# A new instruction order for a spectral filter plus gated feed-forward kernel, with the identity loaded first and a longer warm-up

## The chip, the cores and the metric

The kernel runs on one core of one Trainium2 chip. The metric is the device time of one execution in microseconds, and lower is better. Six executions of the kernel before took 203.97, 203.63, 202.84, 203.64, 203.67 and 202.80 us, so the median is 203.64 us.

## The reference

The input x has 2048 rows of 640 numbers. It is normalised by row, and the normalised matrix goes through two branches that are added to x:

```python
def _A_ref(x, w_r, w_i):
    X = rfft2(x.astype(float32), axes=(-2, -1))     # 2048 x 321 complex
    X = X * (w_r + 1j * w_i)
    return irfft2(X, s=(S, D), axes=(-2, -1)).astype(bfloat16)

def _B_ref(x, w_gate, w_up, w_down):                # F = 1536
    g = einsum("bsd,df->bsf", x, w_gate)
    u = einsum("bsd,df->bsf", x, w_up)
    return einsum("bsf,fd->bsd", g * u, w_down)

xn = _layernorm(A_x)
return A_x + _A_ref(xn, A_w_r, A_w_i) + _B_ref(xn, B_w_gate, B_w_up, B_w_down)
```

## The kernel before

**Steps.** The rows are cut into 16 blocks of 128. The kernel creates 1021 named steps, each a few instructions of one engine, and the names return in the prediction:

- `ld_x`, `ld_gw`, `ld_sm0`, `ld_w`, `ld_wd`, `ld_xr`, `st_out` are loads and stores (line 679 issues all of them). `ld_sm0` is a 128x128 identity matrix, `ld_gw0_1` the first part of the up weights and `ld_gw0_0` that of the gate weights, `ld_w` the filter weights, `ld_wd` the down weights.
- `warm` (L720) and `fill` (L709) on TensorE multiply zeros; nothing reads their results.
- Normalisation: `bn`, `ag` on VectorE for blocks 0 to 5, `sm`, `sq` (L738, L747) on ScalarE for blocks 6 to 15; `sd` takes the square root on ScalarE (L774/775), `rs` the reciprocal on VectorE (L782), `sub` and `mul` apply it.
- `T0` (L818) transposes blocks 0 to 3 on TensorE with the identity, `eT0` copies the result out; the other blocks are transposed by DMA (L806).
- Feed-forward: `GU` multiplies by gate and up weights (L968 for narrow pieces, L948 for pieces of 512 rows), `eG` copies the result from PSUM, `H` multiplies gate and up on VectorE (L984/985), `ACC` multiplies by the down weights (L1206).
- Spectral branch: `S1` to `S5` on VectorE are additions of the forward transform; `R` (L908), `D` (L1026), `C` (L1049) are its products on TensorE, with evictions `eR` and `eD`; `WM` multiplies by the filter on VectorE (three instructions, L1064 and L1067); `NG` and `NS` (L1076/1077, L1084 to 1086) lay out negated copies; `IA` (L1100/1101) and `I` (L1129) are products of the inverse, with evictions `eIA` and `eI`; `V1` to `V5` are its additions on VectorE; `IV` (L1218) adds the last product into the PSUM bank of an `ACC`. `FINA` and `FIN` (L1245, L1227) bring the bank out and add x.

All copies out of PSUM go through one helper, so ScalarE's have line 685 and VectorE's line 686.

**Dependencies that matter.** `D` needs every `eR`, each `R` of a group needs `S5` of that group, `I` needs every `eIA`. A TensorE step that takes one of the eight PSUM banks waits until the step that read the bank's former content is done.

**What sets the order.** The order of the program is not that of the Python loops. `_PLAN` is a fixed list of triples (step number, engine, PSUM bank), made outside of this file. `replay` goes through the list, gives each step to the engine named and each TensorE step its bank; `compute_waits` then derives the semaphore waits. The durations passed to each step only enter the replay's own estimate of times, which decides how waits are merged; they are not instructions. Each engine runs its own list strictly in order, so a step whose input is late holds up everything behind it on that engine. SyncE issues nearly all DMAs in one such list; ScalarE's list begins with two DMAs.

Of the kernel before, what the change touches and what calls it, by code (L numbers as in the profile page):

```python
# [399 lines left out]
def _d_act(n):  # L400
# [4 lines left out]
    (14, 4, -1), (178, 1, -1), (8, 2, -1), (21, 2, -1), (20, 2, -1), (22, 2, -1), (15, 4, -1), (9, 3, -1), (0, 1, -1),  # L405
    (23, 1, -1), (25, 2, -1), (24, 2, -1), (26, 2, -1), (177, 4, -1), (13, 0, 0), (31, 2, -1), (30, 2, -1), (179, 4, -1),
    (180, 4, -1), (16, 4, -1), (27, 0, 2), (11, 0, 4), (32, 2, -1), (28, 1, -1), (12, 0, 5), (33, 1, -1), (17, 4, -1),
    (29, 2, -1), (189, 0, 6), (35, 2, -1), (34, 2, -1), (10, 0, 7), (36, 2, -1), (37, 0, 0), (39, 2, -1), (181, 4, -1),
    (187, 0, 7), (190, 1, -1), (188, 1, -1), (194, 0, 4), (182, 4, -1), (38, 2, -1), (40, 2, -1), (192, 0, 5), (41, 2, -1),
    (199, 0, 2), (183, 4, -1), (191, 2, -1), (42, 2, -1), (197, 0, 3), (195, 1, -1), (202, 0, 4), (43, 1, -1), (50, 2, -1),  # L410
    (45, 2, -1), (184, 4, -1), (44, 2, -1), (46, 2, -1), (193, 1, -1), (49, 2, -1), (198, 1, -1), (204, 0, 5), (47, 0, 3),
    (196, 2, -1), (51, 2, -1), (209, 0, 6), (52, 1, -1), (200, 1, -1), (203, 1, -1), (48, 1, -1), (54, 2, -1), (53, 2, -1),
    (55, 2, -1), (18, 4, -1), (56, 0, 7), (205, 1, -1), (201, 2, -1), (207, 0, 0), (57, 1, -1), (214, 0, 1), (120, 2, -1),
    (206, 2, -1), (212, 0, 7), (121, 2, -1), (217, 0, 2), (185, 4, -1), (210, 1, -1), (208, 1, -1), (70, 1, -1), (211, 2, -1),
    (122, 2, -1), (215, 1, -1), (62, 2, -1), (219, 0, 3), (58, 2, -1), (61, 2, -1), (213, 1, -1), (59, 2, -1), (63, 2, -1),
    (60, 2, -1), (123, 2, -1), (186, 4, -1), (216, 2, -1), (71, 1, -1), (72, 1, -1), (64, 1, -1), (224, 0, 4), (1, 4, -1),
    (19, 4, -1), (222, 0, 5), (220, 1, -1), (218, 1, -1), (2, 4, -1), (65, 2, -1), (124, 2, -1), (229, 0, 6), (73, 1, -1),
    (127, 0, 0), (125, 0, 2), (66, 2, -1), (221, 2, -1), (129, 2, -1), (227, 0, 7), (225, 1, -1), (223, 1, -1), (68, 2, -1),
    (130, 2, -1), (230, 1, -1), (74, 1, -1), (128, 1, -1), (80, 1, -1), (228, 1, -1), (234, 0, 4), (81, 1, -1), (226, 2, -1),
    (82, 1, -1), (232, 0, 5), (83, 1, -1), (131, 2, -1), (231, 2, -1), (237, 0, 6), (233, 1, -1), (75, 2, -1), (3, 4, -1),  # L420
    (84, 1, -1), (235, 1, -1), (132, 2, -1), (239, 0, 7), (76, 2, -1), (78, 2, -1), (4, 4, -1), (238, 1, -1), (240, 1, -1),
    (85, 2, -1), (5, 4, -1), (126, 1, -1), (6, 4, -1), (7, 4, -1), (90, 1, -1), (242, 0, 0), (244, 0, 1), (243, 1, -1),
    (133, 2, -1), (67, 4, -1), (245, 1, -1), (91, 1, -1), (134, 0, 4), (136, 0, 6), (236, 2, -1), (247, 0, 2), (249, 0, 3),
    (69, 4, -1), (77, 4, -1), (92, 1, -1), (250, 1, -1), (248, 1, -1), (86, 2, -1), (241, 2, -1), (93, 1, -1), (94, 1, -1),
    (254, 0, 0), (252, 0, 1), (138, 2, -1), (79, 4, -1), (100, 1, -1), (246, 2, -1), (139, 2, -1), (253, 1, -1), (101, 1, -1),
    (255, 1, -1), (259, 0, 3), (251, 2, -1), (257, 0, 2), (140, 2, -1), (256, 2, -1), (88, 2, -1), (264, 0, 1), (258, 1, -1),
    (95, 2, -1), (87, 4, -1), (262, 0, 0), (102, 1, -1), (260, 1, -1), (269, 0, 2), (103, 1, -1), (135, 1, -1), (104, 1, -1),
    (141, 2, -1), (261, 2, -1), (96, 2, -1), (263, 1, -1), (142, 2, -1), (265, 1, -1), (267, 0, 3), (272, 0, 4), (274, 0, 5),
    (268, 1, -1), (270, 1, -1), (98, 2, -1), (105, 2, -1), (273, 1, -1), (266, 2, -1), (89, 4, -1), (106, 2, -1), (275, 1, -1),
    (97, 4, -1), (149, 0, 0), (108, 2, -1), (277, 0, 3), (137, 1, -1), (271, 2, -1), (143, 0, 4), (110, 1, -1), (150, 1, -1),  # L430
    (99, 4, -1), (147, 0, 6), (278, 1, -1), (282, 0, 2), (144, 1, -1), (151, 2, -1), (283, 1, -1), (279, 0, 0), (280, 1, -1),
    (276, 2, -1), (145, 0, 4), (287, 0, 1), (284, 0, 0), (152, 2, -1), (111, 1, -1), (289, 0, 3), (281, 2, -1), (285, 1, -1),
    (153, 2, -1), (112, 1, -1), (286, 2, -1), (290, 1, -1), (288, 1, -1), (113, 1, -1), (154, 2, -1), (114, 1, -1), (292, 0, 2),
    (291, 2, -1), (294, 0, 3), (115, 2, -1), (155, 2, -1), (299, 0, 0), (293, 1, -1), (146, 1, -1), (297, 0, 1), (295, 1, -1),
    (148, 1, -1), (298, 1, -1), (118, 2, -1), (300, 1, -1), (156, 0, 4), (304, 0, 2), (302, 0, 3), (116, 2, -1), (296, 2, -1),
    (157, 1, -1), (164, 2, -1), (301, 2, -1), (307, 0, 6), (309, 0, 7), (160, 0, 0), (162, 0, 4), (303, 1, -1), (308, 1, -1),
    (107, 4, -1), (165, 2, -1), (305, 1, -1), (109, 4, -1), (158, 0, 2), (306, 2, -1), (117, 4, -1), (310, 1, -1), (314, 0, 6),
    (166, 2, -1), (119, 4, -1), (437, 4, -1), (161, 1, -1), (312, 0, 7), (319, 0, 0), (438, 4, -1), (311, 2, -1), (313, 1, -1),
    (163, 1, -1), (167, 2, -1), (439, 4, -1), (168, 2, -1), (315, 1, -1), (320, 1, -1), (159, 1, -1), (440, 4, -1), (441, 4, -1),
    (317, 0, 1), (316, 2, -1), (442, 4, -1), (318, 1, -1), (322, 0, 7), (324, 0, 6), (443, 4, -1), (175, 0, 4), (173, 0, 2),  # L440
    (174, 2, -1), (323, 1, -1), (327, 0, 7), (444, 4, -1), (169, 0, 0), (171, 0, 2), (176, 1, -1), (321, 2, -1), (325, 1, -1),
    (328, 1, -1), (329, 0, 4), (170, 2, -1), (445, 4, -1), (172, 1, -1), (446, 4, -1), (326, 2, -1), (449, 0, 5), (447, 0, 6),
    (330, 1, -1), (465, 0, 7), (450, 2, -1), (479, 4, -1), (463, 0, 0), (485, 0, 1), (466, 2, -1), (448, 1, -1), (487, 0, 2),
    (332, 0, 3), (451, 0, 4), (457, 0, 5), (334, 0, 6), (452, 2, -1), (464, 1, -1), (453, 3, -1), (467, 0, 7), (480, 4, -1),
    (486, 1, -1), (481, 4, -1), (473, 0, 4), (482, 4, -1), (501, 0, 0), (488, 1, -1), (339, 0, 1), (503, 0, 2), (454, 3, -1),
    (458, 2, -1), (335, 1, -1), (459, 1, -1), (337, 0, 5), (474, 2, -1), (333, 1, -1), (331, 2, -1), (468, 2, -1), (525, 0, 4),
    (475, 3, -1), (483, 4, -1), (460, 3, -1), (455, 0, 3), (484, 4, -1), (495, 0, 6), (745, 4, -1), (502, 1, -1), (469, 3, -1),
    (470, 3, -1), (504, 1, -1), (338, 2, -1), (517, 4, -1), (489, 0, 7), (456, 1, -1), (476, 3, -1), (342, 0, 0), (539, 0, 5),
    (461, 0, 2), (340, 1, -1), (496, 2, -1), (497, 3, -1), (523, 0, 3), (498, 3, -1), (336, 2, -1), (518, 4, -1), (343, 1, -1),
    (505, 0, 6), (344, 0, 1), (519, 4, -1), (462, 1, -1), (490, 2, -1), (520, 4, -1), (521, 4, -1), (511, 0, 0), (524, 2, -1),  # L450
    (522, 4, -1), (471, 0, 7), (477, 0, 2), (349, 0, 3), (526, 1, -1), (540, 1, -1), (541, 0, 4), (555, 4, -1), (491, 1, -1),
    (341, 2, -1), (472, 1, -1), (527, 0, 5), (492, 3, -1), (512, 2, -1), (533, 0, 0), (478, 1, -1), (514, 3, -1), (561, 0, 7),
    (506, 2, -1), (508, 3, -1), (507, 3, -1), (499, 0, 2), (345, 1, -1), (347, 0, 6), (528, 2, -1), (530, 3, -1), (556, 4, -1),
    (542, 1, -1), (557, 4, -1), (558, 4, -1), (559, 4, -1), (563, 0, 1), (579, 0, 5), (534, 2, -1), (493, 0, 4), (549, 0, 0),
    (348, 2, -1), (560, 4, -1), (500, 1, -1), (513, 3, -1), (352, 0, 2), (562, 1, -1), (494, 1, -1), (550, 2, -1), (509, 0, 4),
    (346, 2, -1), (593, 4, -1), (543, 0, 0), (577, 0, 7), (580, 2, -1), (544, 2, -1), (354, 0, 6), (529, 3, -1), (594, 4, -1),
    (515, 0, 5), (350, 1, -1), (535, 2, -1), (536, 3, -1), (601, 0, 3), (595, 4, -1), (564, 1, -1), (353, 1, -1), (571, 0, 2),
    (565, 0, 1), (551, 2, -1), (546, 3, -1), (578, 1, -1), (617, 0, 7), (355, 1, -1), (572, 2, -1), (596, 4, -1), (357, 0, 0),
# [69 lines left out]
def _build(nc, A_x, A_w_r, A_w_i, B_w_gate, B_w_up, B_w_down, out, opts=None):  # L528
    opts = opts or {}
    tabs = _build_tables()  # L530
    es = contextlib.ExitStack()
    with es:
# [171 lines left out]
        for fi in range(opts.get("nfill", 3)):  # L704
            def em_fill(c):
                bk = bank_of(c.t)
                ins = None
                for i in range(4):
                    ins = c.e.matmul(ps[:, bk, 64 * i:64 * i + 64], v_dum[:, 0:128], v_dum[:, 128:192], start=True,  # L709
                                     stop=True)  # L710
# [619 lines left out]
```

## Time and profile before

| | |
|---|---|
| median of 6 executions | 203.64 us |
| profiled execution, its own time | 202.85 us |
| its span, first to last instruction | 200.9 us |
| TensorE busy | 194.6 us (97%) |
| VectorE busy | 172.8 us (86%) |
| ScalarE busy | 128.4 us (64%) |
| GpSimd busy | 37.1 us (18%) |
| first x block landed | 3.5 us |
| first transpose on TensorE | 5.73 us |
| last matmul started | 198.4 us |

The busy times of the engines overlap, so they don't add up to the span. "PE" in the profile is TensorE's matmuls and "PEld" its weight loads, "DVE" is VectorE, "ACT" ScalarE, "POOL" GpSimd, "SPq" SyncE's DMA issues. Times of single instructions count from the start of the span.

### The profile page before, as it was taken

The numbers are of one execution on the slowest core, as the hardware profiler recorded it, in microseconds if no ns is written. First come the engines' busy times: TensorE is split into PE (matmuls) and PEld (weight loads), VectorE is DVE, ScalarE is ACT, GpSimd is POOL, SyncE is SP. The second block draws the span as 40 slices with busy tenths as digits, with TensorE's granted clock in tenths as the row PEclk, the third lists the DMA queues.
The fourth block names the chain that finished last, engine by engine and source line by source line (L and its number), as shares of the span: only waits on it lengthen the run. The fifth ranks groups of instructions, "written<-read, shape, count | busy, mean of one in ns | idle before, by whom it ended". The sixth has DMA issues, their size and how long they took to land.

```text
span 200.9 us, 4556 instructions
## 1 busy us (share of the span) xinstructions
PE 194.6 (97%) x1727; PEld 126.9 (63%) x1749; DVE 172.8 (86%) x396; ACT 128.4 (64%) x284; POOL 37.1 (18%) x116
## 2 busy tenths in 40 slices
PE   7799999999999999999999999999999999999995
PEld 7698644345445465666665566675677766777774
DVE  3899999999999889999969788799699998495813
ACT  3377999999776889999897955652436133312240
POOL 0000000000000009979836736000000000000000
DMA  6999984064028976454663000600024104241322
GB/s 175 303 328 378 382 122 83 0 68 98 0 53 252 193 234 128 109 134 123 154 161 80 17 5 0 206 26 0 6 74 149 38 0 131 65 134 46 121 98 65
DMA packets 29381, 23.81 MB, mean 119 GB/s; under 512 B 10288, under 2 KB 27312, under 8 KB 29232
## 3 DMA queue, kind: packets, MB, share of 16 engines
q1 hardware_dynamic: 28560, 23.16, 43.2%
q10 hardware_dynamic: 800, 0.36, 0.6%
q8 instruction: 14, 0.23, 0.5%
q14 instruction: 7, 0.06, 0.1%
HBM read 18.92 MB, written 2.62 MB: 107 GB/s over the span
## 4 chain that ended last, share of the span: by engine, by line
PE 63%; DVE 15%; ACT 8%; issue 5%; SPq 4%; DMA 4%
PE ps L1206 26%; PE ps L948 23%; ACT arena L685 5%; SPq L679 4%; DMA arena<-in_A_x_dram 4%; DVE arena L984 3%; PE ps L1100 2%; PE ps L1026 2%; PE ps L1101 2%; PE ps L1129 2%; PE ps L1218 2%; PE ps L1049 2%; DVE arena L861 2%; ACT arena L747 2%; ACT arena L738 2%
## 5 line engine op out<-in xcount | busy, mean ns | idle before, releaser
L685 ACT ACTIVATE arena<-ps 128x512 bf16<-128x512 f32 (+7 forms) x225 | 108.7, 528 | 58.0 <-PE ps L1218 30.1
L948 PE MATMUL ps<-arena 128*128 128x512 bf16 x398 | 94.7, 379 | 1.5 <-ACT arena L685 0.3
L948 PEld LDWEIGHTS ps<-arena 128*128 128x128 bf16 x420 | 39.4, 98 | 40.8 <-ACT arena L685 1.9
L1206 PE MATMUL ps<-arena 128*128 128x320 bf16 (+2 forms) x396 | 58.1, 295 | 0.0
L1206 PEld LDWEIGHTS ps<-arena 128*128 128x128 bf16 x396 | 37.7, 98 | 14.5
L1077 POOL TENSOR_SCALAR arena<-arena 128x256 bf16<-128x256 bf16 x15 | 12.9, 860 | 74.9 <-DVE arena L1067 74.9
L1064 DVE TENSOR_TENSOR arena<-ps,arena 128x256 bf16<-128x256 f32 x64 | 24.0, 417 | 2.2 <-PE ps L1049 2.0
L984 DVE TENSOR_TENSOR arena<-arena 128x512 bf16<-128x512 bf16 x42 | 17.9, 426 | 1.9 <-ACT arena L685 1.6
L686 DVE CAST arena<-ps 64x321 bf16<-64x321 f32 (+3 forms) x31 | 17.2, 555 | 2.6 <-PE ps L1101 0.9
L1245 DVE TENSOR_TENSOR arena<-arena 128x640 bf16<-128x640 bf16 x15 | 7.3, 490 | 10.8 <-ACT arena L685 10.8
L968 PE MATMUL ps<-arena 128*128 128x128 bf16 (+1 forms) x160 | 14.0, 246 | 0.6 <-ACT arena L775 0.6
L1100 PE MATMUL ps<-arena 128*128 128x64 bf16 x160 | 13.5, 196 | 0.1
L1101 PE MATMUL ps<-arena 128*128 128x64 bf16 x160 | 13.4, 197 | 0.0
L968 PEld LDWEIGHTS ps<-arena 128*128 128x128 bf16 x160 | 12.3, 98 | 1.7 <-DMA arena<-in_B_w_gate_dram 0.7
L1100 PEld LDWEIGHTS ps<-arena 128*128 128x128 bf16 x160 | 12.0, 114 | 1.7 <-DVE arena L686 0.3
L1086 POOL TENSOR_SCALAR arena<-arena 128x65 bf16<-128x65 bf16 x32 | 12.5, 390 | 0.0
L1101 PEld LDWEIGHTS ps<-arena 128*128 128x128 bf16 x160 | 11.3, 114 | 0.9
L1084 POOL COPY arena<-arena 128x63 bf16<-128x63 bf16 x32 | 8.4, 262 | 11.4 <-DVE arena L1067 11.3
L1026 PEld LDWEIGHTS ps<-arena 128*128 128x128 bf16 x160 | 7.4, 98 | 3.7 <-ACT arena L685 0.4
L1067 DVE TENSOR_TENSOR arena<-ps,arena 128x130 bf16<-128x130 f32 x32 | 9.3, 292 | 0.0
L1218 PE MATMUL ps<-arena 128*128 128x320 bf16 (+2 forms) x33 | 8.6, 295 | 0.0
L1026 PE MATMUL ps<-arena 128*128 128x64 bf16 (+1 forms) x160 | 8.5, 193 | 0.0
(63 smaller groups left out, 205.4 us busy)
## 6 DMA issues: line engine op xcount, KB each, us to landing
arena<-in_A_x_dram SPq DMA_DIRECT2D x20, 160.0 KB, 2.8
out_dram<-arena SPq DMA_DIRECT2D x15, 160.0 KB, 1.8
arena<-in_A_w_r_dram SPq DMA_DIRECT2D x8, 160.5 KB, 3.3
arena<-in_A_w_i_dram SPq DMA_DIRECT2D x8, 160.5 KB, 3.1
arena<-in_B_w_gate_dram SPq DMA_DIRECT2D x4, 320.0 KB, 5.4
arena<-in_A_x_dram SPq DMA_DIRECT2D x1, 1280.0 KB, 9.9
arena<-in_A_w_r_dram SPq DMA_DIRECT2D x14, 80.2 KB, 3.1
arena<-in_A_w_i_dram SPq DMA_DIRECT2D x14, 80.2 KB, 2.8
```

Of the source, the lines that this page charges most:

```text
L685: return c.e.activation(dst, src, _ACTF.Copy)
L686: return c.e.tensor_copy(dst, src)
L948: ins = c.e.matmul(ps[:, bk, :], v_gw[:, w, j, ft, :], v_xt[:, j, rows], start=(j == 0), stop=(j == 4))
L968: ins = c.e.matmul(ps[:, bk, w * n:(w + 1) * n], v_gw[:, w, j, ft, :], v_xt[:, j, rows], start=(j == 0), stop=(j == 4))
L984: return c.e.tensor_tensor(v_ht[:, ft0, rows], v_gbf[:, rr, 0, :], v_gbf[:, rr, 1, :], _OP.mult)
L1026: ins = c.e.matmul(ps[:, bk, k * 64:k * 64 + n], v_uq[:, k, t, :], v_fd[:, k * 128 + w * n: k * 128 + w * n + n], start=True, stop=True)
L1064: c.e.tensor_tensor(dst, xh.unsqueeze(1).to_broadcast([128, 2, 32, 4]), wv, _OP.mult)
L1077: return c.e.tensor_scalar(yg[:, 322:578], yg[:, 834:1090], -1.0, None, _OP.mult)
L1100: c.e.matmul(dst, l1, v_ti[:, q, 0, :], start=True, stop=False)
L1101: ins = c.e.matmul(dst, l2, v_ti[:, q, 1, :], start=False, stop=True)
L1206: ins = c.e.matmul(ps[:, bk, 0:sl3.stop - sl3.start], v_ht[:, ft, a * 128:(a + 1) * 128], v_wd[:, ft, sl3], start=(ft == _FT_ORDER[0]), st ...
L1218: return c.e.matmul(ps[:, bank_of(own), 0:sl3.stop - sl3.start], v_sm[:, 2, :], v_v[:, a, sl3], start=False, stop=True)
```

## The change

Outside of the plan the change is small. There are 40 warm-up matmuls instead of 36. Three filler steps of four small matmuls become one filler step of ten, and every narrow `GU` now depends on it. Four durations of the replay are corrected (`sd` 95 to 187 ns, `mul` 298 to 358 for blocks from 4 on, `NG` on GpSimd 1150 to 820, `warm` 4000 to 4280).

```diff
-        for fi in range(opts.get("nfill", 3)):
-            def em_fill(c):
-                bk = bank_of(c.t)
-                ins = None
-                for i in range(4):
-                    ins = c.e.matmul(ps[:, bk, 64 * i:64 * i + 64], v_dum[:, 0:128], v_dum[:, 128:192], start=True,
-                                     stop=True)
-                return ins
...
-        nwarm = opts.get("nwarm", 9)
+        nfill = opts.get("nfill", 10)
+
+        def em_fill(c):
+            bk = bank_of(c.t)
+            ins = None
+            for i in range(nfill):
+                ins = c.e.matmul(ps[:, bk, 64 * (i % 4):64 * (i % 4) + 64], v_dum[:, 0:128], v_dum[:, 128:192], start=True,
+                                 stop=True)
+            return ins
...
+        nwarm = opts.get("nwarm", 10)
...
-                gu = T("GU_%d_%d" % (ft, b0), "pe", 10.15 * _d_mm(n), em_gu,
+                gu = T("GU_%d_%d" % (ft, b0), "pe", 10.15 * _d_mm(n), em_gu, after=fills,
```

The plan is replaced as a whole; its first lines show the swap on ScalarE's list, where step 0 is `ld_sm0` and step 178 (176 after, since two fillers are gone) is `ld_gw0_1`. The other steps are the same, in another order. By the names of the steps, in the order in which the engines run them:

```
ScalarE before: ld_gw0_1 ld_sm0 sd_0 eT0_0 sd_1 eG_0_1 eG_0_0 eG_1_1 sd_2 ... eG_4_1 eG_4_0 sm6 eG_5_1 eG_5_0 sq6 sm7 sd_4 ...
ScalarE after:  ld_sm0 ld_gw0_1 sd_0 eT0_0 sd_1 eG_0_0 eG_0_1 eG_1_0 sd_2 ... eG_4_0 eG_4_1 eG_5_0 sm6 eG_6_0 sq6 eG_5_1 ...
TensorE before: warm T0_0 fill1 fill2 GU_1_0 fill0 T0_1 GU_0_0 GU_3_0 GU_2_0 ...
TensorE after:  warm T0_0 fill GU_0_0 T0_1 GU_1_0 GU_2_0 GU_3_0 ...
VectorE before: ... S3_1 H_8 rs_5 S4_1 mul6 mul7 rs_6 S5_1 H_9 mul8 H_10 S1_2 ...
VectorE after:  ... rs_5 H_7 S2_1 H_8 S3_1 H_9 S4_1 mul7 S5_1 rs_6 mul6 mul8 H_10 S1_2 ...
SyncE before:   ... ld_w8 (6) ld_w10 (6) ld_wd0 ld_w12 (6) ld_w14 (6) ... st_out0 st_out1 ld_xr4 ld_xr5 ...
SyncE after:    ... ld_w8 (6) ld_wd0 ld_w10 (6) ld_w12 (6) ld_w14 (6) ... st_out0 ld_xr4 st_out1 ld_xr5 ...
```

The engine of a step may change too where several can do it:

| step | ScalarE before, after | VectorE before, after | GpSimd before, after |
|---|---|---|---|
| `eD` (32) | 23, 27 | 9, 5 | |
| `eIA` (32) | 28, 22 | 4, 10 | |
| `NG` (32) | 8, 14 | 9, 10 | 15, 8 |
| `eG` (100) | 93, 89 | 7, 11 | |
| `eR` (16) | 14, 15 | 2, 1 | |
| `eI` (16) | 11, 13 | 5, 3 | |

## The prediction

> **What bounds the kernel now.** I read the page first, then TensorE's waits, the chain that ended last, and the timelines of the stretches where something waits.
>
> ```profile
> span 200.9 us, 4556 instructions
> PE 194.6 (97%) x1727; PEld 126.9 (63%) x1749; DVE 172.8 (86%) x396; ACT 128.4 (64%) x284; POOL 37.1 (18%) x116
> ...
> PE   7799999999999999999999999999999999999995
> DVE  3899999999999889999969788799699998495813
> ACT  3377999999776889999897955652436133312240
> ```
>
> TensorE is busy in every slice, so a new order gains only what TensorE loses to waits. A busy PE can hide a late start, so I laid the 1749 weight loads in program order against the step each load shows where nothing waits: 216 ns for 512 columns, 136 for 320, 56 for 128, 29 for 64. All steps from the first transpose on sum to 188.9 us. That transpose starts at 5.73 and the last matmul ends at 198.6, which is 192.9, so waits and fillers cost about 4.0 us. In order of time: 0.94 in the head (0.72 of it ahead of the first gate/up block at 7.0), 0.18 at 31.3, 0.35 and 0.21 at 38.0 and 39.3, 0.23 at 68.8, about 0.9 between 86 and 97, some 0.6 in 28 ns hiccups inside IA blocks, and almost nothing from 126 on.
>
> ```profile
> PEld ps L948 <- ACT arena L685: 1.9, 6, 0.5
> PEld ps L908 <- DVE arena L895: 0.5, 1, 0.5
> ...
> 87.27 0.12 PEld L1100 LDWEIGHTS ps<-arena 128*128 128x128 bf16 x1 [0.15 <-ACT arena L685]
> 89.07 0.11 PEld L1100 LDWEIGHTS ps<-arena 128*128 128x128 bf16 x1 [0.27 <-DVE arena L686]
> 90.05 0.20 PEld L1026 LDWEIGHTS ps<-arena 128*128 128x128 bf16 x5 [0.35 <-ACT arena L685]
> ```
>
> The first two lines (waits of the weight loads: us in total, times, longest) and the three from the timeline of 85 to 98 show what TensorE waits for: nearly all for a PSUM bank whose eviction (L685 on ScalarE, L686 on VectorE) is late. The exception is L908 <- L895, the last R blocks at 68.8 waiting for VectorE's S5_4.
>
> ```profile
> 67.43 0.69 DVE arena L894
> 68.12 0.61 DVE arena L895
> 68.78 0.73 PE ps L908 x10
> ...
> 29.25 0.17 DVE L782 RECIPROCAL arena<-arena 128x2 f32<-128x2 f32 x1 [0.33 <-ACT arena L774]
> ```
>
> The first three lines are the chain (start, length, line), the last VectorE's timeline. The chain runs on VectorE from 30 to 68.73, then on TensorE. From 9.07 to 68.73 VectorE has one wait over 0.1 us: 0.33 at 29.25, where rs_6 (L782) waits for ScalarE's sd_6. So there are two bounds in series: VectorE up to S5_4, whose start at 9.07 is the landing of block 2 of x, then TensorE's fixed work. TensorE's waits before 68.8 cost nothing by themselves; they only decide whether TensorE is there when S5_4 ends.
>
> ```profile
> 9.07 0.89 DVE L756 BATCH_NORM_STATS2 arena<-arena 128x6 f32<-128x320 bf16 x2 [0.31 <-DMA arena<-in_A_x_dram]
> ```
>
> Columns of a timeline: start, length, engine, line, operation, count, and in brackets the idle time ahead with its releaser. This line is the start of VectorE's unbroken run.
>
> [...] Here all 36 warm-up matmuls ran at 107 ns (1.04 to 5.06) and the first transposes at 5.73 already at 56. [...] ScalarE's 640 packets of up weights (27 ns each) ran from 2.46 to 4.09 almost in one piece, x block 1 mostly behind them, then the identity from 4.05 to 4.65.
>
> **The change part by part.**
>
> *Identity first.* The identity landed at 5.34, but mul0 (VectorE) ended only at 5.61, so T0_0 at 5.73 was released by mul0: no gain. Block 0 of x now shares with 128 packets of 18 ns, 8 per engine, or 8 x 18 = 0.14 us at worst, but no longer meets the first up weights; I take 0 (-0.1 to +0.14). The up weights landed at 4.60 and move back behind 32 KB, to some 5.2; their first reader waits for a VectorE copy ending at 6.87, so 1.7 us cover that. Without that cover each late microsecond would go onto GU_0_0. Total bytes ahead of block 2 of x are the same, and VectorE idles 0.31 before it: the head cannot reach the end of the kernel unless it slips more than 0.31.
>
> *Warm-up and filler.* Four matmuls more: 4 x 107 = 0.43, ending at 5.49 instead of 5.06, still before 5.73: 0, covered by the wait for mul0. Fillers go from 2 x 4 + 4 to one block of 10. Ten end about 6.5, before the 7.0 of GU_0_0: 0. The dropped four at 7.57 stood in TensorE's wait for mul1 (ends 7.66): 0. If the clock rose late in a run, more warm-up would help; the profiled execution shows no sign of that, since T0_0 ran at 56 ns. This is at least a possible reason for the two groups of times (below).
>
> *VectorE's order up to S5_4.* The set of instructions is the same, so the sum is too. What changes is the 0.33: S5_1 (0.66 start to start) and H_9 (0.32) now stand ahead of rs_6, and mul6 (0.36) behind it, so VectorE gets there 0.62 later. Summing ScalarE's queue from 17.05 (the x load that lets sm6 start) puts sd_6 at the same place in both orders: one wide eviction (0.48) moves into ScalarE's idle 1.44 us before 17.05 and another takes its place. The wait of 0.33 to 0.40 becomes a slack of 0.24. At the other places where VectorE reads a ScalarE result the slack by the same sums is no worse than -0.01, so nothing new should wait. S5_4 ends 0.35 earlier (0 to 0.5).
>
> *Is TensorE there?* The same steps stand ahead of the first of R_12 to R_15. TensorE came 0.23 before S5_4 ended although it had lost 0.18 + 0.35 + 0.21 to ScalarE's evictions since 31; eR_0, for which it waited at 31.3, now stands twelve places earlier on ScalarE. It needs only 0.12 of those 0.74 to be there. Gain kept: -0.35.
>
> *Stretch of D, C and IA (69 to 126).* Counted over the two orders, ScalarE gets 4 more eD (2 x 0.435 each), 6 more NG (0.414), 2 eI (0.706) and 1 eR (0.712), and loses 6 eIA (0.437) and 4 wide eG (0.599): 3.48 + 2.48 + 1.41 + 0.71 - 2.62 - 2.40 = +3.1 us. VectorE: -4 x 0.98 + 1 x 0.24 + 6 x 0.485 + 4 x 0.683 - 2 x 0.82 - 0.82 = -0.5. GpSimd: -7 x 0.86 = -6.0. ScalarE is nearly full from 69 to 98 (27.5 of 29 us busy) and has 6.8 us free from 98 to 126. Its queue summed up to the eviction or NG that each C or IA waits for leaves about 1.9 us of TensorE work until 86 in both orders; from 88 to 96 it leaves 2.4 to 3.3 where the smallest (over both engines) was 1.9 before. Of the 0.9 lost there I take half back: -0.5, with ends -0.9 (all) and +0.8 (as much again). The 28 ns hiccups stay.
>
> *SP's queue.* ld_wd0, which waits for IA_0 to IA_9 (last at 92.0), moves ahead of the six w10 loads, and w12 and w14 queue behind. These were issued from 90.04 on and had landed by 96.4; now they begin near 92.7 and land near 99. Their reader WM_21 started at 103.2: about 4 us of cover, then w12 (1.1 us later) lands near 104 for WM_24 at 107.3. 0. The alternation of output stores and x reloads meets slack too: 0.
>
> *From 126 on.* TensorE waits for nothing. I added up the new VectorE order V1 to V5 with the FIN adds among them against TensorE's work up to each first IV: 1.1 us of slack at IV_0, 3 to 5 later. The tail (last IV to last store, 198.4 to 200.9) is unchanged: 0. If the 1.1 failed, each microsecond would land on the end.
>
> Sum: -0.35 - 0.5 = -0.85. The profiled execution took 202.85 (span 200.9 and 1.95 around it), so 202.0. But the runs shown lie in two groups, 202.8 (two) and 203.6 to 204.0 (four), and the profiled one is in the faster; the median is 0.79 above it. Keeping that share: 202.8.
>
> **Rivals.** (a) *Both groups fold into the faster one*, as the longer warm-up and earlier identity make the head steadier: 202.0, down to 201.4 with all of the 0.9. For: the groups are 0.8 apart, discrete, and the head is where the clock and the DMA queues decide. Against: nothing in the one trace shows it. (b) *No change*: half the 0.35 is lost because a new wait appears on VectorE (H_9's slack is -0.01), and ScalarE's waits between 75 and 97 only move: 203.2 to 203.7. For: the 1.9 us margins until 86 are the same as before. (c) *Slower*: ScalarE heads its queue with NG steps (14 instead of 8), each waiting for a WM (three VectorE steps, 0.87 to 0.96) with eD, eG and eIA behind it, and those hold PSUM banks. It decides once ScalarE loses more than its 1.9 us margin: with four such blocks at 0.9 it loses 3.6, TensorE 1.7, and the 0.5 is not gained: 203.64 - 0.35 + 1.7 = 205.0. Against: POOL loses 6 us, and ScalarE's sums leave more room after 88.
>
> **How the numbers follow.** Forecast 0.42 (202.3 to 203.2), (a) 0.23, (b) 0.22, (c) 0.13. A difference below 0.3% (203.03 to 204.25 is "same") can't be told from none here. Faster: most of the forecast's and all of (a)'s: 0.61. Same: (b) and the forecast's upper end: 0.26. Slower: 0.13. The range leaves out the end of (a) and most of (c): 201.5 to 204.2.
>
> **What would show it.** Right: no wait over 0.1 at rs_6, the first of R_12 to R_15 near 68.4, and waits between 86 and 97 of about 0.4. Wrong: ScalarE idle ahead of NG (L1076, one line lower after the change) while TensorE waits for L686; a wait of WM for a weight load; matmuls of the first gate/up blocks at 107 ns; or S5_4 still at 68.7.

## The result, and the profile after

The changed kernel takes 202.42 us in the median (31 executions, 202.13 to 203.13). The kernel before, run beside it on the same chip, takes 203.15 (66 executions, 202.62 to 204.07). The ratio is 0.9963, with a 95% interval of 0.9954 to 0.9971: 0.37% faster. The forecast of 202.8 (201.5 to 204.2) holds, but the gain is not made up as the forecast had it.

The profiled executions are 202.85 us before (span 200.9) and 202.43 after (span 200.6). From the page of the changed kernel, the busy times, the slices and the chain that ended last:

```profile
span 200.6 us, 4555 instructions
PE 194.8 (97%) x1731; PEld 127.4 (63%) x1751; DVE 171.8 (86%) x396; ACT 131.0 (65%) x291; POOL 31.5 (16%) x109
...
PE   7799999999999999999999999999999999999995
...
DVE  3799999999999969999988797599989889809933
ACT  3379999999958599999999875654043134351321
...
PE 75%; DVE 14%; DMA 3%; issue 3%; ACT 3%; SPq 1%
```

The work has moved between engines as counted: ScalarE +2.6 us, VectorE -1.0, GpSimd -5.6. The chain now lies on TensorE for 75% of the span and on VectorE for 14%.

VectorE's timeline of the changed kernel, first where its unbroken run starts, 9.07 before:

```profile
8.10 0.56 DVE L686 COPY arena<-ps 128x384 bf16<-128x384 bf16 x2 [0.55 <-PE ps L819]
9.31 0.89 DVE L757 BATCH_NORM_STATS2 arena<-arena 128x6 f32<-128x320 bf16 x2 [0.65 <-DMA arena<-in_A_x_dram]
```

VectorE is ready at 8.66 and waits 0.65 us for block 2 of x (0.31 before): the run starts 0.24 later, whatever came earlier in the head. Then the same timeline at the place where `rs_6` waited 0.33 us before (line 783 after the change; lines from the filler step on are one higher):

```profile
28.92 0.42 DVE L895 SCALAR_TENSOR_TENSOR arena<-arena 128x256 bf16<-128x256 f32 x1
29.26 0.42 DVE L896 SCALAR_TENSOR_TENSOR arena<-arena 128x256 bf16<-128x256 f32 x1
29.59 0.16 DVE L783 RECIPROCAL arena<-arena 128x2 f32<-128x2 f32 x1
29.67 0.79 DVE L800 TENSOR_SCALAR arena<-arena 128x640 bf16<-128x640 bf16 x2
```

No bracket stands behind any of the four: the wait is gone. The chain of the changed kernel between 66 and 70 us, where before `S5_4` handed over to the last R blocks:

```profile
67.59 1.03 PE ps L949 x4
68.62 0.90 PE ps L909 x15
```

The chain passes through TensorE alone there. `S5_4` ends at 68.37 (68.73 before), and the first of R_12 to R_15 starts at 68.49 (68.78 before): TensorE now comes about 0.06 us later than it could. Behind that, the timeline of TensorE's weight loads in the changed kernel between 84 and 126 us, all lines with a wait:

```profile
85.16 0.76 PEld L949 LDWEIGHTS ps<-arena 128*128 128x128 bf16 x5 [0.20 <-DVE arena L1068]
86.18 0.10 PEld L1050 LDWEIGHTS ps<-arena 128*128 128x128 bf16 x1 [0.26 <-ACT arena L685]
...
114.49 0.11 PEld L1101 LDWEIGHTS ps<-arena 128*128 128x128 bf16 x1 [0.18 <-DVE arena L1068]
```

The three waits of before in this stretch (0.15, 0.27 and 0.35 at 87.27, 89.07 and 90.05) are gone, and three others stand there: a gate/up block and an IA block behind VectorE's `WM`, a C block behind ScalarE. A bracket is idle time of the weight loads and not TensorE's loss (from 86 to 98 its matmuls are busy for 11.86 of the 12 us, with the 0.26 in a bracket there), so I laid the weight loads against their undisturbed steps again, as for the forecast: between 69 and 126 us TensorE loses 0.92 us after the change and 0.94 before, by my count. The stalls moved and their sum stayed; the last column of the next table says the same without such a count.

One table carries the comparison of all kernels. "VectorE" is the start of its unbroken run (the `bn` of block 2), S1_0 and S5_4 are VectorE's steps, R is the start of the first of R_12 to R_15, "last" the start of the last matmul (both by their weight loads); one profiled execution each, in us.

| kernel | VectorE | S1_0 | S5_4 ends | S1_0 to S5_4 | R | last | R to last |
|---|---|---|---|---|---|---|---|
| before | 9.07 | 13.31 | 68.73 | 55.42 | 68.78 | 198.34 | 129.56 |
| changed | 9.31 | 13.48 | 68.37 | 54.90 | 68.49 | 198.08 | 129.59 |
| e1_identity_first | 9.38 | 13.62 | 68.55 | 54.93 | 68.60 | 198.17 | 129.57 |
| e2_warm40 | 9.61 | 14.36 | 69.84 | 55.48 | 69.89 | 199.44 | 129.55 |
| e3_head_after | 9.11 | 13.27 | 68.16 | 54.88 | 68.27 | 197.80 | 129.53 |
| e4_tail_after | 9.71 | 14.17 | 69.46 | 55.29 | 69.52 | 199.09 | 129.57 |
| e5_rs6_only | 9.16 | 13.40 | 68.69 | 55.30 | 68.75 | 198.26 | 129.52 |
| e6_both_starts | 9.29 | 13.53 | 68.55 | 55.02 | 68.61 | 198.13 | 129.52 |
| e7_start_undone | 9.04 | 13.20 | 68.13 | 54.93 | 68.25 | 197.84 | 129.59 |
| e8_four_warmups | 9.15 | 13.31 | 68.42 | 55.11 | 68.54 | 198.14 | 129.60 |
| e9_up_first | 9.20 | 13.36 | 68.29 | 54.93 | 68.41 | 198.03 | 129.62 |
| e10_warm36 | 9.10 | 13.27 | 68.16 | 54.90 | 68.28 | 197.87 | 129.59 |
| e11_best | 9.01 | 13.18 | 68.22 | 55.04 | 68.34 | 197.89 | 129.55 |
| e12_changed_again | 8.84 | 13.01 | 67.91 | 54.90 | 68.02 | 197.60 | 129.58 |

Each execution also has a recorded span and a mean granted clock, so a median can be taken apart. Over 144 executions of before (those beside the experiments) and 41 of the changed kernel (its 31 and the 10 of e12), means: time 203.085 and 202.430; span 201.065 and 200.629; so time outside of the span 2.02 and 1.80. Of the spans, 55 of 144 are 201.2 us or longer before, and 2 of 41 after; the shorter ones average 200.80 and 200.60. The difference of 0.655 us splits into three parts of like size:

- shorter spans among themselves: 200.80 - 200.60 = 0.20;
- fewer long spans: 201.065 - 200.80 = 0.265 before, 200.629 - 200.60 = 0.03 after, so 0.23;
- outside of the span: 2.02 - 1.80 = 0.22.

The limit of 201.2 is my choice; the sum does not depend on it, and with a limit from 201.0 to 201.4 the first part is 0.18 to 0.24 and the second 0.26 to 0.19. The 144 and the 41 are not from the same chips. On the chip of the result, where no span of the 66 executions of before is on record, the means differ by 0.76, and 31 of the 66 lie above 203.3 us, against 44 of the 144. So the long spans probably weigh more there.

### The profile page after: what moved, and what is told of

The parts are those of the page before. It is cut to its first block, busy times and chain, and to the rows that moved or that the text cites. A ratio compares the mean times of both kernels' runs of the same rounds, so it can differ in the third digit from the quotient of the medians.

```text
span 200.6 us, 4555 instructions
## 1 busy us (share of the span) xinstructions
PE 194.8 (97%) x1731; PEld 127.4 (63%) x1751; DVE 171.8 (86%) x396; ACT 131.0 (65%) x291; POOL 31.5 (16%) x109
## 4 chain that ended last, share of the span: by engine, by line
PE 75%; DVE 14%; DMA 3%; issue 3%; ACT 3%; SPq 1%
PE ps L949 34%; PE ps L1207 26%; DMA arena<-in_A_x_dram 3%; ACT arena L685 2%; PE ps L1130 2%; PE ps L1102 2%; PE ps L1101 2%; PE ps L1219 2%; PE ps L1027 2%; PE ps L1050 2%; PE ps L909 2%; DVE arena L757 2%; DVE arena L861 1%; DVE arena L862 1%; DVE arena L800 1%
## 5 line engine op out<-in xcount | busy, mean ns | idle before, releaser
L685 ACT ACTIVATE arena<-ps 128x512 bf16<-128x512 f32 (+6 forms) x226 | 109.1, 528 | 60.4 <-PE ps L1219 20.6
L686 DVE CAST arena<-ps 128x512 bf16<-128x512 f32 (+3 forms) x32 | 17.6, 566 | 4.5 <-PE ps L1102 1.9
L1078 POOL TENSOR_SCALAR arena<-arena 128x256 bf16<-128x256 bf16 x8 | 6.9, 864 | 75.5 <-DVE arena L1068 75.5
L1050 PE MATMUL ps<-arena 128*128 128x321 bf16 x32 | 8.6, 301 | 0.0
```

The source lines that it names most:

```text
L685: return c.e.activation(dst, src, _ACTF.Copy)
L686: return c.e.tensor_copy(dst, src)
L1050: return c.e.matmul(ps[:, bank_of(c.t), 0:_LP], v_tf[:, q, :], v_a[:, ar, 324 * g:324 * g + _LP], start=True, stop=True)
```

## The experiments

Theory and rivals: (T) the gain comes from the order up to the last R and from the stretch after it; (a) it comes from a steadier start; (b) the stretch after it gives nothing. All kernels compute the full output. Orders are given by the names of the steps. The clock of an execution is the mean that its record grants.

### e1_identity_first: the two DMAs on ScalarE's list, in the kernel before

```diff
- ScalarE: ld_gw0_1 ld_sm0 sd_0 eT0_0 ...
+ ScalarE: ld_sm0 ld_gw0_1 sd_0 eT0_0 ...
```

> The kernel before with one edit: the identity is loaded ahead of the first up weights on ScalarE's queue; everything else as before. Theory A (the new order of steps carries the gain): median within 0.1 us of before's 203.15, lowest execution at 202.6; S5_4 still ends near 68.7, the wait at rs_6 stays at 0.3. Theory B (the start of the DMA queues carries it, since block 0 of x landed 0.30 us earlier after the change): median 0.3 to 0.7 lower, and fewer executions above 203.3, where half of before's lie.

Measured: 202.66 us (17 executions), before 202.96, ratio 0.9975 (0.9961 to 0.9988). Only 1 of the 17 lies above 203.3 us, against 19 of 59 of before. In the profiled execution VectorE starts 0.31 later than in before, and `S5_4` still ends 0.18 earlier. VectorE's timeline at `rs_6`:

```profile
28.42 0.80 DVE L799 TENSOR_SCALAR arena<-arena 128x640 bf16<-128x640 bf16 x2
29.13 0.16 DVE L782 RECIPROCAL arena<-arena 128x2 f32<-128x2 f32 x1
```

The wait of 0.33 us is gone, against theory A, although the order is the old one. VectorE comes later, and `sd_6` starts 0.16 earlier (28.77 instead of 28.93), since the x load that lets `sm6` start landed at 16.75 instead of 17.03. So in the old order this wait depends on when two x loads land, and it is not the same in every execution.

### e2_warm40: forty warm-up matmuls, in the kernel before

```diff
-        nwarm = opts.get("nwarm", 9)
+        nwarm = opts.get("nwarm", 10)
```

> The kernel before with 40 warm-up matmuls instead of 36, nothing else. Theory A: median within 0.1 us of 203.15. Theory C (a longer warm-up keeps TensorE's clock from coming up late in part of the executions): median 0.3 to 0.7 lower, with few executions above 203.3; the profiled one, which lies near the lowest, changes little.

Measured: 202.81 us (23), ratio 0.9984 (0.9973 to 0.9995), and again 1 of 23 above 203.3. The profiled execution happens to be that one, 204.06 us with a mean clock of 0.992. TensorE's timeline in it:

```profile
6.17 0.44 PE L818 MATMUL ps<-arena 128*128 128x128 bf16 x5 [1.15 <-DVE arena L798]
...
7.43 0.92 PE L968 MATMUL ps<-arena 128*128 128x128 bf16 x10 [0.59 <-ACT arena L775]
...
8.38 0.72 PE L818 MATMUL ps<-arena 128*128 128x128 bf16 x5
```

The same steps in before, with the clock up:

```profile
5.76 0.44 PE L818 MATMUL ps<-arena 128*128 128x128 bf16 x5 [0.70 <-DVE arena L798]
...
7.02 0.72 PE L968 MATMUL ps<-arena 128*128 128x128 bf16 x10 [0.59 <-ACT arena L775]
...
7.72 0.45 PE L818 MATMUL ps<-arena 128*128 128x128 bf16 x5
```

In e2 the first transpose ran at full clock (0.44 us for five), the second at half (0.72), and the first gate/up block between them (0.92, against 0.72) across the change. The clock had been up and fell back. The table by stretch of the same execution (stretch, its length, then busy time and count of TensorE's matmuls and weight loads, VectorE, ScalarE and GpSimd, the granted clock, the DMA share and GB/s):

```profile
5.50:9.00 3.50, 2.24 (x34) 2.18 (x34) 2.47 (x10) 1.06 (x3) 0.00 (x0) 0.83 1.17 304
9.00:12.00 3.00, 3.00 (x37) 3.00 (x36) 2.54 (x9) 1.07 (x4) 0.00 (x0) 0.63 1.19 295
12.00:17.00 5.00, 5.00 (x72) 4.74 (x70) 4.86 (x16) 3.65 (x10) 0.00 (x0) 1.00 1.10 354
```

The clock records in the trace give full clock from 4.39 to 7.81, half from 7.81 to 11.22, then full. In the 3.42 us up to 7.81 TensorE idled 1.15 + 0.59 us; block 0 of x had landed at 3.93 instead of 3.51.

This tells what some of the long executions may be. One period of 3.41 us at half clock in 201 us makes a mean of 1 - 1.71 / 201 = 0.9915. Of before's 144 executions 16 have a mean of 0.991 or 0.992, and all 16 took 203.43 us or more. Where in the execution the half clock stood is on record for e2's profile alone. Of the changed kernel's 41 none has such a mean, but one of e3's 11 and one of e9's 10 do, with the new order and 40 warm-up matmuls.

### e3_head_after and e4_tail_after: the two orders spliced at the first D

```diff
  e3: changed kernel
- order from the first D on: as changed
+ order from the first D on: as before
  e4: kernel before
- order from the first D on: as before
+ order from the first D on: as changed
```

PSUM banks were renamed at the seam.

> The changed kernel's start, warm-up, filler and order up to the last R, then the order and engine choices of the kernel before from the first D on (banks renamed so that the freed ones come first). Theory A with the whole gain ahead of D, as the two traces say (R 0.29 earlier, last matmul 0.26 earlier): as fast as the changed kernel, 202.4, ratio to before 0.996. If the stretch of D, C and IA gave the 0.5 that was forecast: 202.9.

> The reverse: the kernel before up to the last R, with its 36 warm-ups, three fillers and up weights first, then the changed kernel's order from the first D on. Theory A with the gain ahead of D: median within 0.15 us of 203.15. If the stretch of D, C and IA gave 0.5: 202.65.

Measured: before 202.96; e3 202.31 us (11), ratio 0.9965 (0.9944 to 0.9987), all of the changed kernel's gain. e4 203.39 (22), ratio 1.0012 (0.9998 to 1.0025), none of it. The column "R to last" says why: 129.53 and 129.57, as in before and in the changed kernel. Of these two orders from D on, neither is worth more than the other, and the time from R to the last matmul is 129.52 to 129.62 us in all fourteen profiles.

e4's profiled execution (203.92) is a long one of another kind. TensorE's timeline, then VectorE's:

```profile
7.23 1.22 PE L968 MATMUL ps<-arena 128*128 128x128 bf16 x10 [0.25 <-ACT arena L775]
...
8.48 0.72 PE L818 MATMUL ps<-arena 128*128 128x128 bf16 x5
```

```profile
9.24 0.56 DVE L686 COPY arena<-ps 128x384 bf16<-128x384 bf16 x2 [1.47 <-PE ps L818]
9.71 0.87 DVE L756 BATCH_NORM_STATS2 arena<-arena 128x6 f32<-128x320 bf16 x2
```

Here the clock was at half until 10.3 us and never up before. The first gate/up block takes 1.22 us instead of 0.72, `T0_1` comes at 8.48 instead of 7.72, VectorE waits 1.47 us for it in its copy, and its unbroken run starts at 9.71 instead of 9.07, not held by x but by TensorE. `S1_0` is 0.86 late, and R is 0.74 late with it. The profile page grants this execution a full clock, since the first clock record in its trace stands at 10.32, with the rise; a late rise is seen in the length of the steps alone.

### e5_rs6_only: VectorE's steps around `rs_6`, in the kernel before

```diff
- VectorE: ... mul6 mul7 rs_6 S5_1 H_9 mul8 ...
+ VectorE: ... mul7 S5_1 H_9 rs_6 mul6 mul8 ...
```

> The kernel before with one edit in VectorE's list: S5_1 and H_9 ahead of rs_6, mul6 behind it. Order theory (the 0.35 comes from this wait): the wait at rs_6 goes, S5_4 ends 0.35 earlier, but TensorE came only 0.23 ahead of it before, so the last R starts 0.23 to 0.35 earlier and the lowest execution falls from 202.45 to about 202.2; the start is not touched, so executions above 203.3 stay as frequent as before (a third to a half) and the median lies about 0.3 lower, 202.7. Rival (the 0.35 comes from other moves of the new order): within 0.1 of before.

Measured: 202.94 us (14), ratio 1.0008 (0.9993 to 1.0023). VectorE's timeline:

```profile
29.57 0.42 DVE L984 TENSOR_TENSOR arena<-arena 128x512 bf16<-128x512 bf16 x1 [0.25 <-ACT arena L685]
29.91 0.16 DVE L782 RECIPROCAL arena<-arena 128x2 f32<-128x2 f32 x1
```

The wait at `rs_6` is gone, and `H_9` in front of it waits 0.25 us for its ScalarE eviction: S1_0 to S5_4 is 55.30, 0.12 better than before and not 0.52. In the changed kernel `H_9` runs at 27.56 without a wait, since ScalarE has done that eviction before. So VectorE's move alone does not pay; that ScalarE's new order is all that it needs is not tested by itself.

### e6_both_starts: e1 and e2 together, in the kernel before

```diff
- ScalarE: ld_gw0_1 ld_sm0 ...     nwarm 9
+ ScalarE: ld_sm0 ld_gw0_1 ...     nwarm 10
```

> The kernel before with identity first and 40 warm-up matmuls, the order of everything else as before. Start theory ([...] together they do no more than one): 202.65, few executions above 203.3, lowest at about 202.3. If the two add up: 202.4, and then the new order would have brought nothing.

Measured: 202.83 us (14), ratio 0.9996 (0.9981 to 1.0011), with 1 of 14 above 203.3. This is no measured gain, where e1 alone showed one. The kernel before, run beside e5 to e8, had only 10 of 43 above 203.3 and a median of 202.87. What e1, e2 and e6 have in common is the count: 3 of 54 with a span of 201.2 or longer, against 55 of 144, and the shorter spans average 200.73 (200.80 in before). The start-up edits remove long executions and give at most 0.07 us to the others.

### e7_start_undone and e8_four_warmups: the new order with the old start, and almost no warm-up

```diff
  e7: changed kernel
- ScalarE: ld_sm0 ld_gw0_1 ...     nwarm 10
+ ScalarE: ld_gw0_1 ld_sm0 ...     nwarm 9
  e8: changed kernel
-        nwarm = opts.get("nwarm", 10)
+        nwarm = opts.get("nwarm", 1)
```

> The changed kernel with up weights first and 36 warm-up matmuls again; one filler block of ten and the new order stay. Start theory: lowest execution still near 202.2, but a third or so of the executions are again 0.7 to 1.0 higher; median 202.5 to 202.9. Order theory alone (start is worth nothing): 202.4 with none above 202.9.

> The changed kernel with 4 warm-up matmuls instead of 40. Clock theory: TensorE is idle from about 1.5 to 5.4 us, so its first transposes and gate/up blocks run at 107 ns a step in every execution, and the last R starts about 1 us later: 203.3 to 203.9. Rival (TensorE is early enough that the head's clock is hidden behind VectorE): within 0.2 of 202.4.

Measured: e7 203.25 us (14), ratio 1.0004 (0.9984 to 1.0024); e8 203.04 (14), ratio 1.0011 (0.9994 to 1.0028). Both have 8 of 14 spans of 201.2 or longer. The other six of e7 average 200.57, as short as the changed kernel's 200.60. So the new order needs one of the start-up edits to show its gain in the median, and with a good start it has the gain without them. The one filler of ten stays in every kernel with the new order, so these runs don't separate it from the order. Three of e7's eight carry the mean clock of 0.991 or 0.992; none of e8's does.

e8's profiled execution (202.50) gives the price of a late clock from the other side. TensorE's timeline, then VectorE's:

```profile
6.84 1.22 PE L969 MATMUL ps<-arena 128*128 128x128 bf16 x10 [0.24 <-ACT arena L776]
```

```profile
8.64 0.56 DVE L686 COPY arena<-ps 128x384 bf16<-128x384 bf16 x2 [1.15 <-PE ps L819]
9.15 0.89 DVE L757 BATCH_NORM_STATS2 arena<-arena 128x6 f32<-128x320 bf16 x2
```

The first gate/up block runs at half clock here too, but the clock rises near 8.6 (steps of 107 ns up to 8.40, of 56 from 8.59), the copy ends at 9.19, about when block 2 of x lands (9.12), and VectorE starts at 9.15. Half clock until 8.6 costs the start of VectorE's run next to nothing, until 10.3 it costs 0.6 there and 0.7 at R. Still, e8's six shorter spans average 200.90, 0.3 above those of the changed kernel; that rest is not explained.

### e9_up_first, e10_warm36, e11_best, e12_changed_again: which start-up edit, and could both orders be mixed

```diff
  e9: changed kernel
- ScalarE: ld_sm0 ld_gw0_1 ...
+ ScalarE: ld_gw0_1 ld_sm0 ...
  e10: changed kernel
-        nwarm = opts.get("nwarm", 10)
+        nwarm = opts.get("nwarm", 9)
  e11: e3_head_after
- ScalarE: ld_sm0 ld_gw0_1 ...
+ ScalarE: ld_gw0_1 ld_sm0 ...
  e12: changed kernel, unedited
```

> The changed kernel with the up weights first on ScalarE's queue again; 40 warm-up matmuls stay. If the longer warm-up alone keeps TensorE's clock up: few executions above 202.9, and because block 2 of x then lands 0.24 earlier (9.04 instead of 9.29) and starts VectorE's unbroken run, the median is 0.1 to 0.25 below the changed kernel, 202.2. If the earlier identity is what keeps it up: a third or more of the executions near 203.3 to 204.0, median 202.5 to 203.2.

> The changed kernel with 36 warm-up matmuls; the identity stays first. If the earlier identity (block 0 of x 0.3 earlier, first transpose at 5.4) is enough: as the changed kernel, 202.4. If the longer warm-up is needed: a third or more of the executions 0.7 to 1.0 higher, median 202.5 to 203.2.

> A try at something better: the kernel of e3 (new order up to the last R, before's order from D on) with the up weights first and 40 warm-ups. If the longer warm-up alone is enough: 202.0 to 202.2, below both kernels. If not: like e7, 202.5 to 203.2.

> The changed kernel unedited, on the chip of e9 to e11, to compare with: median 202.4, ratio to before 0.996, nearly none above 202.9.

Measured, with before at 203.15 us: e9 202.38 (10), ratio 0.997 (0.995 to 0.999); e10 202.29 (21), 0.9964 (0.9952 to 0.9976); e11 202.41 (14), 0.9963 (0.9952 to 0.9975); e12 202.30 (10), 0.9955 (0.9939 to 0.9972). Spans of 201.2 or longer: 1 of 10, 2 of 21, 0 of 14 and 0 of 10. Either start-up edit alone is enough in the new order to make long executions rare, and both together show no more. No mixture beats the changed kernel.

## Why the prediction was right or wrong

**The total.** Forecast 202.8, measured 202.42, inside the likeliest case's own range. The forecast took 0.85 off a median of six that happened to be high, 203.64; over 66 executions it is 203.15, and the gain is 0.73. That it came so near is luck: the terms behind it were others.

**The step that failed** is "Of the 0.9 lost there I take half back: -0.5", for the stretch of D, C and IA. Measured: 0.0. TensorE's losses between 69 and 126 us are 0.94 before and 0.92 after, and R to last matmul does not move with the order (129.53 with before's order in e3, 129.57 with the new one in e4). I had summed ScalarE's queue up to each eviction and found more room from 88 us on. That room is real for those places, but ScalarE has 11.6 of 12 us busy between 86 and 98 in the changed kernel (11.7 before), and two of the three new waits (0.20 and 0.18 us) are behind VectorE's `WM`, which my sums of ScalarE's queue left out. The mark that I had set, waits of about 0.4 between 86 and 97, was met (0.26 at 86.18) and proved nothing, since the loss stood just outside of that stretch. Rival (b) had said it: the waits only move.

**Head, "-0.35".** The mechanism was right: the wait at `rs_6` disappears, and with the new order S1_0 to S5_4 takes 54.88 to 55.11 whatever the start of VectorE's run (8.84 to 9.31), against 55.42 in before. e3, which has this part and the start-up edits, has the whole gain, and e7's six shorter spans, without those edits, are as short as the changed kernel's. In the profiled pair R comes 0.29 earlier; that is 0.52, less 0.17 because VectorE reached S1_0 later in this execution (block 2 of x landed at 9.29 instead of 9.04), less 0.06 for TensorE's being late at R. Over the executions with shorter spans the gain is 0.20. It is smaller than 0.52 because in the old order the wait at `rs_6` is not always there: in e1 and e6 VectorE began 0.2 to 0.3 later, `sd_6` came 0.16 to 0.17 earlier, and S1_0 to S5_4 took 54.93 and 55.02 without a wait at `rs_6`. The profile of before, from which the 0.35 was read, had an early block 2 and a late `sd_6`. That the wait is all of the 0.20 is argued, not shown. "Is TensorE there?" was answered too generously by 0.06 us.

**Start-up edits, "0".** Right for what the forecast priced, the profiled execution. There the identity and the earlier `T0_0` (5.42 instead of 5.73) gave nothing, since VectorE's run starts with block 2 of x. The bound of -0.1 to +0.14 on block 0 of x was too narrow on the side of a gain: it landed 0.3 us earlier. The up weights landed at 5.48, forecast 5.2, under the cover named. The forecast's fillers to 6.5 ended at 6.2. With the same bytes ahead of it, block 2 of x still landed 0.25 later; where VectorE waits for it, its landing varies from 8.82 (e12) to 9.36 us (e1) between the profiles.

**The groups of times: rival (a) rather than "Keeping that share".** The forecast kept before's share of slower executions. It fell from 55 of 144 to 2 of 41 and gave 0.23 us of the mean. That the start-up edits do this is shown by the counts of e1, e2, e6, e9 and e10. The reason named in (a), the start and the clock, is shown for the profiled executions of e2 and e4, and the mean clocks of 0.991 and 0.992 fit it for 16 of before's 55. That the other 39 are late rises as in e4 is argued from e7 and e8, not shown; a late landing of x, as in e2 (block 0 at 3.93), remains a rival for them. That the moment of the rise varies is measured: with 40 warm-up matmuls the clock records show it at 4.28 us in e11 and at 6.51 in e3; with 36 and the same order of steps in the head, the first transposes ran at full clock at 5.76 in before, and the rise came at 10.32 in e4.

**Not foreseen: 0.22 us outside of the span.** The time around the span is 2.02 us in before, 2.00 to 2.05 in e1, e2, e5 and e6, 1.79 to 1.83 in every kernel with the new order up to R, and 2.16 in e4. So it follows the program, not the start-up edits. In the traces of before, the changed kernel, e3 and e4 the first recorded instruction starts at 0.24 us alike. Behind the last instruction the DMA records differ: in before, e1, e2, e5 and e6 the instruction queue (q14) fetches one more packet of 8 KB, 1.75 to 1.81 us after the end of the span, and in no kernel with the new order up to R. But e4, with the largest time, has no such packet either, so the fetch alone does not explain it. What it is stays open.

**SP's queue and the end, "0".** Right: R to last is unchanged with six weight loads moved, and no wait at the filter's `WM` steps came of it. **Rival (c)**, slower through ScalarE's NG steps, did not happen: with 14 instead of 8 of them there, TensorE lost nothing more.

So the sum of -0.85 met a measured -0.73 by other terms: -0.20 for the head instead of -0.35, 0 for the stretch instead of -0.5, and -0.23 for the start and -0.22 around the span, both costed at 0 (these three are from the means over 144 and 41 executions, which differ by 0.655; the 0.73 is from the medians of the 66 and 31).

## What to carry to other kernels

When a wait for one engine is removed by moving steps of another, check the step that comes to stand there: in e5 a wait of 0.25 us appeared one instruction earlier. Sums over a nearly full engine's queue did not turn into a gain here while its busy time stayed the same (11.6 of 12 us against 11.7): the stalls changed place, and TensorE lost 0.92 us instead of 0.94. Before a median is explained by one profile, look at the spread of the executions: almost a quarter-microsecond of this gain is in neither of the two profiles, and it came from edits that were priced at zero from the profile. A start-up step need not be faster to be worth having; it was enough here that long executions became rare (1 of 17 above 203.3 us in e1, against 19 of 59 in before).

## What the runs showed of the hardware

In e2 the clock fell back in the head after the warm-up had raised it, at 4.39 us. In the 3.42 us up to 7.81 TensorE idled 1.74 us, the longest piece 1.15; then it ran 3.41 us at half clock (0.72 us for five transposes instead of 0.44), busy without a break. In e11 and e9, with the rise at 4.28 and 4.58 us, TensorE idled 1.46 and 1.51 us of the 3.41 us behind it, the longest piece 0.73 and 0.78, and the clock stayed up. What separates these executions from e2 they don't settle.

The first rise was late in e4, at 10.32 us. TensorE had idled 0.80 us between the warm-up and the first transpose and 0.25 us ahead of the first gate/up block, and it was busy without a break from 7.23 on. In e7 the piece ahead of the first transpose was 0.68 and the rise came at 6.40; in e10 it was 0.41, with the rise at 6.12; in before it was 0.70, and the transposes behind it, at 5.76, ran at full clock already. Whether that piece decides is not shown. It was shorter with the identity first (0.35 in e1 against 0.70 in before, 0.41 in e10 against 0.68 in e7, 0.20 in the changed kernel), but not with 40 warm-up matmuls alone (1.15 in e2, 0.78 in e9).

How many executions are long, in the new order: 8 of 14 with 36 warm-up matmuls and the up weights first (e7), 8 of 14 with four and the identity first (e8), 2 of 21 with 36 and the identity first (e10), 1 of 10 with 40 and the up weights first (e9).
